# A decode attention and FFN kernel on one core: values of one unit loaded before the FFN's weights, an FFN that is column-tiled throughout and leaves the bank of PV after its first layer, and the output turned inside the next key transpose

## Chip, core and metric

The kernel runs on one NeuronCore of a Trainium2 chip. The metric is the device time of one execution in microseconds. The time is about 1.8 us longer than the span of the profile, which goes from the first to the last instruction. In the views below, PE is the matrix engine (TensorE), PEld its loads of weights, DVE the vector engine, ACT the scalar engine, and SP the engine that issues the large loads.

Executions of the kernel before do not all take the same time, so each run has a state, fast or slow. Verdicts compare fast runs alone. Where I quote all runs, I say so.

## The reference, cut to what matters

```python
x  = A_x                                   # (2, 1, 448), bf16
xn = layernorm(x)
q  = (xn @ wq)                             # 16 heads of 256, two to a key/value head
k, v = the last 2048 of 8192 cached rows   # 8 key/value heads, 256 wide, 2 batches
s  = softmax(q k^T / 16) v @ wo            # attention, then the output projection
g  = silu(relu(xn @ w1) @ w2)              # FFN, 448 -> 1792 -> 448
out = x + s * g
```

The operands are read once: keys 16.8 MB, values 16.8, wq and wo 3.7 each, w1 and w2 1.6 each. The profile counts 44.11 MB read from HBM. There is one token per batch, so there is little arithmetic per byte.

## The kernel before

The work is done in four units u (batch u // 2, half of the heads u % 2). Each unit has 4 MiB of keys and 4 MiB of values. Per unit the PE transposes the keys (`do_T`, 16 chunks of four 128x128 transposes, evacuated by DVE and ACT in turn), multiplies them with q (`do_S`), and after a softmax multiplies the probabilities with the values (`do_PV`). Then `attend` scales and turns the result. At the end 128 matmuls with wo form the output (`O` below). K2 means the keys of unit 2, V2 its values. `obk` and the five `tb` are PSUM banks, where PE leaves its results: `obk` takes PV, the FFN and O, the `tb` take the transposed keys.

```python
def load_v(u):
    deps = [st.get(("PV", u - 2))] + ([st["q_mm"]] if u == 1 else [])
    d_v[u] = pr.dma(SP, vbuf[u % 2][:, :], kv_src(u, A_v_cache), deps)
# ... cut
def softmax(u, fill=()):       # meanwhile() emits the next piece of `fill` on the PE
    meanwhile()
    # DVE: row maximum; PE: transpose it (rmT); DVE: maximum over chunks
    meanwhile()
    # DVE copy; PE: broadcast (bias); DVE: shift
    meanwhile()
    # ACT: Exp; PE: transpose the probabilities (Pt); DVE: copy to pt
    meanwhile()
    # PE: sums (gs); DVE: reciprocal rs
# ... cut
def attend(u):                 # DVE: o_sb = obk * rs; PE: turn o_sb; DVE: at_exp
# ... cut
def do_H(u):                   # u = 0, 1: half of the FFN's first layer, 7 matmuls 4 x 448 into obk
# ... relu on DVE; do_hT: 7 transposes into obk; do_F: 56 matmuls 2 x 112 into obk; silu from obk
# ... cut
scores(0)
load_k(2); load_v(1)
softmax(0)
scores(1)
load_k(3)
softmax(1, value_parts(0)); attend(0)
scores(2)
st["w1"] = pr.dma(SP, ..., w1_src, [st["T", 2]])     # cut
st["w2"] = pr.dma(SP, ..., w2_src, [st["T", 2]])     # cut
load_v(2)
softmax(2, value_parts(1)); attend(1)
load_v(3)
scores(3)
# wo in pieces of 12, 12, 4, 2, 2 of its 32 blocks, each after T of unit 3
softmax(3, [lambda: do_H(0), lambda: do_H(1), do_hT, do_F])
for u in (2, 3):
    do_PV(u); attend(u)
# ... O: for j in range(32): four matmuls of block j; then out = O * g + x on DVE, and two stores
```

All large loads go through one queue, in program order, and in the traces they land in that order.

Of the kernel before, what the change touches and what calls it, by code (L numbers as in the profile page):

```python
# [5 lines left out]
BF = mybir.dt.bfloat16  # L6
F32 = mybir.dt.float32
ACT = mybir.ActivationFunctionType
ALU = mybir.AluOpType
AX = mybir.AxisListType  # L10

PE, DVE, ACTE, SP, POOL = "pe", "dve", "act", "sp", "pool"
# [64 lines left out]
def bass_recurrent_scan__sliding_block_cached__dense_activation_relu__decode_kernel(  # L77
# [11 lines left out]
    B, Sq, D = A_x.shape  # L89
    _, HKV, SK, DH = A_k_cache.shape  # L90
# [8 lines left out]
    NU = 4  # L99
    NT = 64  # L100
    NCHUNK = NT // 4
    UW = NT * DH
    SLOTS = 7
    HC = HD // 2
    FC = DFF // 2
    WO_PARTS = [12, 12, 4, 2, 2]
    NCOL = D // 4
# [6 lines left out]
    with es:  # L114
        pr = _Prog(nc, es)

        def named(name, shape, dt):
            return es.enter_context(nc.sbuf_tensor(name, shape, dt))
# [4 lines left out]
        def view(t, off, dims, n=128, p0=0, pstep=1):  # L123
            width = t.shape[1]
            return bass.AP(t, p0 * width + off, [[width * pstep, n]] + dims)

        ident = named("ident", [128, 128], BF)
# [17 lines left out]
        xr = named("xr", [128, SLOTS * 4], BF)  # L145
        q_n = named("q_n", [128, 512], BF)
        qz = named("qz", [128, 2 * NU * 64], BF)
        h_n = named("h_n", [128, FC], BF)
        h_sb = named("h_sb", [128, 28], BF)
        x_c = named("x_c", [128, NCOL], BF)  # L150
        ea = named("ea", [128, NCOL], F32)
# [30 lines left out]
        def kv_src(u, cache):  # L182
            b, v = divmod(u, 2)
            return cache[b, 4 * v:4 * v + 4, SK - W:SK, :].rearrange("h (r t) d -> r h (t d)", t=NT)
# [16 lines left out]
        def load_k(u):  # L201
            d_k[u] = pr.dma(SP, kbuf[u % 2][:, :], kv_src(u, A_k_cache), [st.get(("T", u - 2))])

        def load_v(u):
            deps = [st.get(("PV", u - 2))] + ([st["q_mm"]] if u == 1 else [])
            d_v[u] = pr.dma(SP, vbuf[u % 2][:, :], kv_src(u, A_v_cache), deps)

        load_k(0)
        d_wq = pr.dma(SP, wq_sb[:, 0:SLOTS * HC], wq_src)
# [19 lines left out]
            out=sd[0:B, 0:1], in0=st2[0:B, 1:2], scalar1=EPS, scalar2=None, op0=ALU.add), [v_ag])  # L229
        a_sd = pr.op(ACTE, lambda e: e.activation(sd[0:B, 1:2], sd[0:B, 0:1], ACT.Sqrt), [v_ve])  # L230
        v_rs = pr.op(DVE, lambda e: e.reciprocal(rstd[0:B, :], sd[0:B, 1:2]), [a_sd])
        for e2 in range(2):
            v_xn = pr.op(DVE, lambda e, e2=e2: e.tensor_scalar(  # L233
                out=view(xg, 128 - 127 * e2, [[256, 4], [128, 2], [2, 64]], n=B),
                in0=view(x_sb, 3 * e2, [[1, 4], [0, 2], [SLOTS, 64]], n=B),
                scalar1=st2[0:B, 0:1], scalar2=rstd[0:B, 0:1],
                op0=ALU.subtract, op1=ALU.mult), [v_rs])
# [22 lines left out]
        def mm(out_ap, lhsT, rhs, start, stop=False, **kw):  # L260
            return lambda e: e.matmul(out_ap, lhsT=lhsT, rhs=rhs, start=start, stop=stop,  # L261
                                      skip_group_check=True, **kw)
# [30 lines left out]
        def do_S(u, g):  # L293
            deps = [st["q"]] + ([st.get(("shift", u - 1))] if g == 0 else [])
            for par in range(2):
                lo = 64 * (2 * u + par) + 24 - 8 * g
                for i in range(4):
                    o = pr.op(PE, mm(sbk[32 * i:32 * i + 32, :], qz[:, lo:lo + 32], view(kt[4 * g + i], par, [[2, 512]]),
                                     g == 0 and par == 0, g == 3 and par == 1, tile_position=(0, 32 * i)),
                              deps + [evac[NCHUNK * u + 4 * g + i]])  # L300
                    deps = []
            for i in range(4):
                last_S[NCHUNK * u + 4 * g + i] = o
            st["S", u] = o
# [48 lines left out]

        def do_PV(u, gs=range(4)):
            bank, src, p = obk, vbuf[u % 2], pt[u % 2]
            deps = [d_v[u], st["pt", u], a_z, st["obk"]]
            for g in gs:
                for a in range(2):
                    for i in range(4):
                        lo = (16 * g + 4 * i + 2 * a) * DH  # L360
                        o = pr.op(PE, mm(bank[32 * i:32 * i + 16, :],
                                         p[:, 256 * a + 64 * i + 16 * g:256 * a + 64 * i + 16 * g + 16], src[:, lo:lo + 2 * DH],
                                         g == 0 and a == 0, g == 3 and a == 1, tile_position=(0, 32 * i)), deps)
                        deps = []
            st["PV", u] = o

        def attend(u):
            b, v = divmod(u, 2)
            ob = st["obk"] = pr.op(DVE, lambda e: e.tensor_scalar(  # L369
                out=o_sb[:, :], in0=obk[:, :], scalar1=rs[:, u:u + 1], scalar2=None, op0=ALU.mult),  # L370
                [st["PV", u], st["rs", u], st.get(("oT", u - 1))])
            deps = [ob, v_fold, st["mbk"]]
            for dhi in range(2):
                for tp in range(2):
                    o = pr.op(PE, mm(mbk_ap(136 + 8 * dhi, 8), o_sb[:, 256 * tp + 128 * dhi:256 * tp + 128 * dhi + 128],
                                     fold[:, 8 * tp:8 * tp + 8], tp == 0, tp == 1), deps)
                    deps = []
            st["oT", u] = o
            st["at", u] = st["mbk"] = pr.op(DVE, lambda e: e.tensor_tensor(
                out=view(at_exp, 128 * b + 64 * v, [[8, 8], [4, 2], [1, 4]]),  # L380
                in0=view(mbk, 136, [[1, 8], [8, 2], [0, 4]]),
                in1=view(qmask, 0, [[0, 8], [0, 2], [1, 4]]), op=ALU.mult), [o, v_qm])
# [21 lines left out]
                        view(qz, 256 * b + 64 * r + 24, [[128, 2], [2, 4], [1, 2]]),  # L404
                        view(mb16, 128 * r + b, [[2, 2], [32, 4], [256, 2]])), [o, p_qz])

        def do_H(u):
            deps = [st["w1"], a_z, st["obk"]]
            for s in range(SLOTS):
                lo = s * FC + u * (FC // 2)  # L410
                o = pr.op(PE, mm(obk[0:4, 0:FC // 2], xr[:, 4 * s:4 * s + 4], w1_sb[:, lo:lo + FC // 2],
                                 s == 0, s == SLOTS - 1), deps)
                deps = []
            st["h_n"] = st["obk"] = pr.op(DVE, lambda e: e.tensor_scalar(  # L414
                out=h_n[0:4, u * (FC // 2):(u + 1) * (FC // 2)], in0=obk[0:4, 0:FC // 2],
                scalar1=0.0, scalar2=None, op0=ALU.max), [o])

        def do_hT():
            deps = [st["h_n"]]
            for j in range(7):  # L420
                o = pr.op(PE, mm(obk[:, 4 * j:4 * j + 4], view(h_n, j, [[7, 128]], n=4), ident[0:4, 0:4], j == 0), deps)
                deps = []
            st["hT"] = st["obk"] = pr.op(DVE, lambda e: e.tensor_copy(
                view(h_sb, 0, [[2, 7], [14, 2], [1, 2]]), view(obk, 0, [[4, 7], [2, 2], [1, 2]])), [o])

        def do_F():
            deps = [st["w2"], st["hT"]]
            for f in range(14):
                for i in range(4):
                    lo = W2_AT + f * D + i * NCOL  # L430
                    o = pr.op(PE, mm(obk[32 * i:32 * i + B, 0:NCOL], h_sb[:, 2 * f:2 * f + 2], w2_sb[:, lo:lo + NCOL],
                                     f == 0, f == 13, tile_position=(0, 32 * i)), deps)
                    deps = []
            a_e = pr.op(ACTE, lambda e: e.activation(ea[:, :], obk[:, 0:NCOL], ACT.Exp, scale=-1.0), [o])
            v_d = pr.op(DVE, lambda e: e.tensor_scalar(
                out=ea[:, :], in0=ea[:, :], scalar1=1.0, scalar2=None, op0=ALU.add), [a_e])
            v_rc = pr.op(DVE, lambda e: e.reciprocal(tmp[:, :], ea[:, :]), [v_d])  # L437
            st["g"] = st["obk"] = pr.op(DVE, lambda e: e.tensor_tensor(
                out=g_sb[:, :], in0=obk[:, 0:NCOL], in1=tmp[:, :], op=ALU.mult), [v_rc])

        def scores(u):
            for i in range(NCHUNK):
                do_T(u, i)
                if u and i >= 6 and i % 4 == 2:
                    do_S(u, (i - 6) // 4)
            if u == 0:
                do_q()
                for g in range(3):
                    do_S(u, g)
            do_S(u, 3)  # L450

        def value_parts(u):
            return [lambda g=g: do_PV(u, (g,)) for g in range(4)]

        scores(0)
        load_k(2)
        load_v(1)
        softmax(0)
        scores(1)
        load_k(3)  # L460
        softmax(1, value_parts(0))
        attend(0)
        scores(2)
        st["w1"] = pr.dma(SP, w1_sb[:, 0:W2_AT], w1_src, [st["T", 2]])
        st["w2"] = pr.dma(SP, w2_sb[:, W2_AT:W2_AT + 14 * D].rearrange("p (hf f) -> p hf f", hf=2), w2_src,
                          [st["T", 2]])
        load_v(2)
        softmax(2, value_parts(1))
        attend(1)
        load_v(3)  # L470
        scores(3)
        d_wo = []
        j0 = 0
        for n in WO_PARTS:
            d_wo.append((j0, pr.dma(SP, wo_sb[:, j0 * D:(j0 + n) * D], wo_src[:, j0 * D:(j0 + n) * D], [st["T", 3]])))
            j0 += n
        softmax(3, [lambda: do_H(0), lambda: do_H(1), do_hT, do_F])
        for u in (2, 3):
            do_PV(u)
            attend(u)  # L480
        for b in range(2):
            m_at = pr.op(PE, mm(mbk_ap(256 + 32 * b, 32), at_exp[:, 128 * b:128 * b + 128],
                                fold[:, :], True, True), [st["at", NU - 1], v_fold, st["mbk"]])
# [4 lines left out]
        for j in range(32):  # L488
            deps = deps + [landed.get(j)]
            for i in range(4):  # L490
# [3 lines left out]
                deps = []  # L494
# [38 lines left out]
```

## Time and profile before

| before | us |
|---|---|
| first timed runs | 116.78, 112.79, 112.93 (median 112.93) |
| profiled run (slow) | 116.5, span 114.7 |

The first lines of the page of the kernel before. The rows are 40 equal slices of the span. PE and DMA are busy tenths, PEclk is the granted TensorE clock in tenths.

```profile
span 114.7 us, 1850 instructions
...
PE   0010399966259999656999965699996525879390
...
PEclk9999999999955799996569999656999998555555
DMA  5889999989899899899898998999898998998000
```

The DMA engines are at least 80% busy from the second slice to the 37th. PE is not, and its clock falls to half four times.

The end of the chain of waits (the work that ended last, in order of time; columns are start, length, what):

```profile
97.85 3.62 PE obk L261 x31
...
101.49 0.76 DVE o_sb L369
...
102.57 3.55 PE obk L261 x27
...
106.14 0.76 DVE o_sb L369
...
108.54 3.18 PE obk L261 x128
```

This is PE work and DVE work end to end: PV of unit 2 (97.85), its output scale (101.49), PV of unit 3 (102.57), its scale, then O from 108.54. No load is in this end of the chain.

The DMA stream, by stretches (columns: stretch and its length, busy time of each engine with the number of instructions, granted clock, DMA share, GB/s):

```profile
4.00:40.00 36.00, 21.64 (x180) 17.75 (x180) 15.90 (x40) 13.64 (x16) 0.00 (x0) 0.91 1.01 437
40.00:80.00 40.00, 33.27 (x286) 23.69 (x282) 19.92 (x41) 15.43 (x19) 0.00 (x0) 0.83 1.01 432
80.00:100.00 20.00, 14.06 (x178) 8.16 (x174) 9.38 (x21) 4.91 (x8) 0.00 (x0) 0.92 0.97 414
...
104.00:105.00 1.00, 1.00 (x12) 0.29 (x8) 0.00 (x0) 0.00 (x0) 0.00 (x0) 0.50 0.98 378
105.00:106.00 1.00, 1.00 (x12) 0.14 (x4) 0.00 (x0) 0.00 (x0) 0.00 (x0) 0.50 0.66 247
106.00:107.00 1.00, 0.14 (x6) 0.05 (x2) 0.75 (x1) 0.00 (x0) 0.00 (x0) 0.50 0.30 113
```

The DMA share is near 1.0 for a hundred microseconds. It falls only from 105 us on, and the last bytes come between 106 and 107.

From the start of each issue and its time to landing, K2 lands at 52.3, V1 at 62.0 and K3 at 71.7 us: 4.19 MB every 9.7 us, that is 432 GB/s. V2 lands at 89.0, V3 at 98.7 and the last piece of wo at about 107.4 (issued at 87.7, 19.7 us to landing). So two things end almost together in this kernel: the stream at 107.4, and the PE chain that reaches O at 108.5. The five loads of wo in the timeline, and the last two of them in the page's list (KB each, us from issue to landing):

```profile
85.89 2.24 SPq L36 DMA_DIRECT2D kbuf<-in_A_wo_dram  x5
...
kbuf<-in_A_wo_dram SPq DMA_DIRECT2D x2, 224.0 KB, 19.7
```

### The profile page before, as it was taken

What the parts mean: (1) busy time and instruction counts of PE and PEld (TensorE: products, weight loads), DVE (VectorE), ACT (ScalarE), POOL (GpSimd) and SP (SyncE); (2) the same over time, 40 slices, a digit from 0 to 9 for tenths busy, and PEclk for the clock granted to TensorE, in tenths of its full rate; (3) what the DMA queues carried; (4) which work ended last, traced back from release to release, by engine and by line L of the source; (5) the groups of instructions that cost most, each with busy time, mean ns of one, the idle gap of its engine ahead of it and who ended that gap; (6) DMA issues with size and microseconds to landing.
All of it is one profiled execution on the core that took longest, in us unless ns stands there. A gap on an engine that the chain in (4) does not pass through costs nothing.

```text
span 114.7 us, 1850 instructions
## 1 busy us (share of the span) xinstructions
PE 78.0 (68%) x810; PEld 54.3 (47%) x810; DVE 49.0 (43%) x111; ACT 35.5 (31%) x42; POOL 2.0 (2%) x11
## 2 busy tenths in 40 slices
PE   0010399966259999656999965699996525879390
PEld 0000399922149776124977612497772224322280
DVE  2091046852623555535445553544553465030401
ACT  1900047960023766020376602036670021000000
POOL 6000000000000000000000000000000000000000
PEclk9999999999955799996569999656999998555555
DMA  5889999989899899899898998999898998998000
GB/s 172 377 366 446 423 480 390 456 366 543 366 411 503 366 469 446 360 514 403 377 514 377 440 468 339 409 493 428 377 520 377 423 491 345 399 409 338 34 6 1
DMA packets 2475, 44.22 MB, mean 385 GB/s; under 512 B 290, under 2 KB 548, under 8 KB 932
## 3 DMA queue, kind: packets, MB, share of 16 engines
q1 hardware_dynamic: 2440, 44.11, 90.4%
q8 instruction: 6, 0.10, 0.3%
q10 hardware_dynamic: 28, 0.00, 0.0%
q14 instruction: 1, 0.01, 0.0%
HBM read 44.11 MB, written 0.00 MB: 385 GB/s over the span
## 4 chain that ended last, share of the span: by engine, by line
PE 64%; DVE 18%; DMA 11%; ACT 3%; issue 2%
PE tb L281 35%; PE obk L261 14%; DMA kbuf<-in_A_k_cache_dram 11%; PE sbk L261 8%; PE mbk L261 4%; DVE s_sb L331 3%; ACT e_sb L336 3%; DVE o_sb L369 2%; DVE rm L314 2%; DVE kt L289 2%; PE mbk L341 2%; DVE h_n L414 1%; PE mbk L319 1%; DVE mrow L322 1%; DVE tmp L437 1%
## 5 line engine op out<-in xcount | busy, mean ns | idle before, releaser
L281 PE MATMUL tb<-ident_f,kbuf 128*128 128x128 f32 x256 | 40.9, 331 | 5.5 <-DMA kbuf<-in_A_k_cache_dram 5.5
L281 PEld LDWEIGHTS tb<-ident_f,kbuf 128*128 128x128 f32 x256 | 38.0, 176 | 9.6 <-DMA kbuf<-in_A_k_cache_dram 5.6
L291 ACT ACTIVATE kt<-tb 128x1024 bf16<-128x1024 bf16 x28 | 27.7, 1023 | 32.2 <-PE tb L281 32.2
L289 DVE COPY kt<-tb 128x1024 bf16<-128x1024 bf16 x36 | 24.8, 691 | 26.4 <-PE tb L281 26.4
L261 PE MATMUL obk<-vbuf,pt 128*16 128x512 bf16 x128 | 12.5, 504 | 1.6 <-DVE rs L351 1.6
L261 PE MATMUL sbk<-kt,qz 128*32 128x512 bf16 x128 | 11.0, 393 | 1.6 <-DVE kt L289 1.1
L336 ACT ACTIVATE e_sb<-s_sb 128x512 bf16<-128x512 f32 x4 | 2.5, 629 | 24.7 <-DVE s_sb L331 24.7
L261 PEld LDWEIGHTS obk<-vbuf,pt 128*16 128x16 bf16 x128 | 3.3, 105 | 6.0 <-issue 5.0
L369 DVE TENSOR_SCALAR o_sb<-obk,rs 128x512 bf16<-128x512 f32 x4 | 3.0, 742 | 7.0 <-PE obk L261 7.0
L341 PE MATMUL mbk<-ident,e_sb 128*128 128x128 bf16 x16 | 1.8, 243 | 5.7 <-ACT e_sb L336 5.7
L261 PE MATMUL mbk<-ident,xg 2*128 2x2 bf16 x7 | 0.3, 163 | 7.4 <-DVE xg L233 7.4
L261 PEld LDWEIGHTS sbk<-kt,qz 128*32 128x32 bf16 x128 | 2.7, 94 | 5.6 <-issue 2.1
L341 PEld LDWEIGHTS mbk<-ident,e_sb 128*128 128x128 bf16 x16 | 1.0, 106 | 6.9 <-ACT e_sb L336 6.9
L314 DVE TENSOR_REDUCE rm<-sbk 128x4 f32<-128x512 f32 x4 | 2.7, 686 | 3.6 <-PE sbk L261 3.6
L319 PE MATMUL mbk<-ident_f,rm 128*1 128x128 f32 x4 | 1.1, 270 | 4.3 <-DVE rm L317 4.3
L346 DVE COPY pt<-mbk 128x512 bf16<-128x512 bf16 x4 | 1.7, 424 | 5.1 <-PE mbk L341 5.1
L261 PEld LDWEIGHTS mbk<-ident,xg 2*128 2x128 bf16 x7 | 0.3, 100 | 7.4 <-DVE xg L233 7.4
L261 PE MATMUL mbk<-fold,o_sb 128*128 128x8 bf16 x16 | 1.1, 173 | 3.5 <-DVE o_sb L369 3.5
L261 PEld LDWEIGHTS mbk<-fold,o_sb 128*128 128x128 bf16 x16 | 0.7, 108 | 5.5 <-DVE o_sb L369 5.5
L261 PE MATMUL obk<-kbuf,at 128*2 128x112 bf16 x128 | 3.2, 298 | 0.3 <-DVE at L484 0.3
L319 PEld LDWEIGHTS mbk<-ident_f,rm 128*1 128x1 f32 x4 | 0.3, 79 | 6.3 <-DVE rm L317 6.3
L261 PEld LDWEIGHTS obk<-kbuf,at 128*2 128x2 bf16 x128 | 2.9, 124 | 0.4 <-DVE at L484 0.4
(67 smaller groups left out, 41.9 us busy)
## 6 DMA issues: line engine op xcount, KB each, us to landing
kbuf<-in_A_k_cache_dram SPq DMA_DIRECT2D x4, 4096.0 KB, 27.8
vbuf<-in_A_v_cache_dram SPq DMA_DIRECT2D x4, 4096.0 KB, 32.0
vbuf<-in_A_wq_dram SPq DMA_DIRECT2D x1, 3584.0 KB, 20.3
kbuf<-in_B_w_dram SPq DMA_DIRECT2D x2, 1568.0 KB, 11.5
kbuf<-in_A_wo_dram SPq DMA_DIRECT2D x2, 1344.0 KB, 17.5
kbuf<-in_A_wo_dram SPq DMA_DIRECT2D x1, 448.0 KB, 19.6
kbuf<-in_A_wo_dram SPq DMA_DIRECT2D x2, 224.0 KB, 19.7
x_c<-in_A_x_dram ACTq DMA_DIRECT2D x2, 0.9 KB
```

The source lines that it names most:

```text
L261: return lambda e: e.matmul(out_ap, lhsT=lhsT, rhs=rhs, start=start, stop=stop, skip_group_check=True, **kw)
L281: o = pr.op(PE, lambda e, n=n, lo=lo: e.matmul(bank_f[:, n * 128:(n + 1) * 128], lhsT=src_f[:, lo:lo + 128], rhs=ident_f[:, :], start=True ...
L289: evac[n_th] = pr.op(DVE, lambda e: e.tensor_copy(dst[:, :], bank[:, :]), deps)
L291: evac[n_th] = pr.op(ACTE, lambda e: e.activation(dst[:, :], bank[:, :], ACT.Copy), deps)
L314: v = pr.op(DVE, lambda e: e.tensor_reduce(out=rm4[:, :], in_=view(sbk, 0, [[1, 4], [4, 128]]), axis=AX.X, op=ALU.max), [st["S", u]])
L319: m = st["rmT", u] = pr.op(PE, lambda e: e.matmul(mbk_ap(0, 128, 1), lhsT=rm[:, :], rhs=ident_f[:, :], start=True, stop=True, is_transpose ...
L322: v = pr.op(DVE, lambda e: e.tensor_reduce(out=mrow[0:1, :], in_=view(mbk, 0, [[1, 8], [8, 16]], n=1), axis=AX.X, op=ALU.max, negate=True) ...
L331: v = st["shift", u] = pr.op(DVE, lambda e: e.scalar_tensor_tensor(out=view(s_sb, 0, [[4, 128], [1, 4]]), in0=view(sbk, 0, [[4, 128], [1, ...
L336: a = st["exp", u] = pr.op(ACTE, lambda e: e.activation(e_sb[:, :], s_sb[:, :], ACT.Exp, accum_out=ssum[:, 0:1]), [v, st.get(("Pt", u - 1) ...
L341: o = pr.op(PE, lambda e, j=j: e.matmul(mb16[:, 512 + 128 * j:640 + 128 * j], lhsT=e_sb[:, 128 * j:128 * j + 128], rhs=ident[:, :], start= ...
L346: v = st["pt", u] = pr.op(DVE, lambda e: e.tensor_copy(view(pt[u % 2], 0, [[256, 2], [16, 16], [8, 2], [1, 8]]), view(mb16, 512, [[256, 2] ...
L369: ob = st["obk"] = pr.op(DVE, lambda e: e.tensor_scalar(out=o_sb[:, :], in0=obk[:, :], scalar1=rs[:, u:u + 1], scalar2=None, op0=ALU.mult) ...
```

## The change

The intent was to shorten the PE chain after the last keys. V2 is loaded before w1 and w2, so that PV of unit 2 can fill the gaps of softmax 3, as PV of units 0 and 1 fill those of softmax 1 and 2. The FFN moves behind that softmax. Its first layer and its transposes become column-tiled (four groups of 32 columns side by side, as the second layer already was). The first layer stays in `obk`, but the transposes and the second layer go to two of the `tb` banks, so that the silu runs beside PV of unit 3. V3 comes in two loads. The turn of units 0 and 1 moves behind the fourth chunk of the next T, so that T need not wait for the output scale. An early dummy Exp moves the load of the Exp table.

```diff
-        def load_v(u):
+        def load_v(u, cuts=(0, NT)):        # one DMA per cut; do_PV waits for the one it needs
...
+        pr.op(ACTE, lambda e: e.activation(tmp[0:B, 0:1], st2[0:B, 0:1], ACT.Exp), [a_sd])
...
-        def attend(u):
+        def attend_scale(u):                # DVE part
+        def attend_turn(u):                 # PE turn and at_exp
...
-        def do_H(u):                        # 7 matmuls 4 x 448, called twice
+        def do_H():                         # 28 matmuls 4 x 224, tile_position=(0, 32 * i)
...                                          # do_hT into tb[0], do_F into tb[1], not into obk
         def scores(u):
             for i in range(NCHUNK):
                 do_T(u, i)
...
+                if i == 3 and u > 1:
+                    attend_turn(u - 2)
...
-        def value_parts(u):
-            return [lambda g=g: do_PV(u, (g,)) for g in range(4)]
+        def values(u):
+            return [lambda gs=gs: gs and do_PV(u, gs) for gs in ((0,), (), (1, 2), (3,))]
...
-        softmax(1, value_parts(0))
-        attend(0)
+        softmax(1, values(0))
+        attend_scale(0)
+        load_v(2)
         scores(2)
         st["w1"] = ...; st["w2"] = ...
-        load_v(2)
-        softmax(2, value_parts(1))
-        attend(1)
-        load_v(3)
+        softmax(2, values(1))
+        attend_scale(1)
+        load_v(3, (0, 48, 64))
         scores(3)
...
-        softmax(3, [lambda: do_H(0), lambda: do_H(1), do_hT, do_F])
-        for u in (2, 3):
-            do_PV(u)
-            attend(u)
+        softmax(3, values(2))
+        attend_scale(2)
+        do_H()
+        attend_turn(2)
+        do_hT()
+        do_F()
+        do_PV(3)
+        attend_scale(3)
+        attend_turn(3)
```

More of the change, by code (lines that the diff above doesn't have):

```diff
@@ L147, in bass_recurrent_scan__sliding_block_cached__dense_activation_relu__decode_kernel @@
         qz = named("qz", [128, 2 * NU * 64], BF)
-        h_n = named("h_n", [128, FC], BF)
+        h_n = named("h_n", [128, FC // 4], BF)
         h_sb = named("h_sb", [128, 28], BF)
@@ L202, in load_k @@
             d_k[u] = pr.dma(SP, kbuf[u % 2][:, :], kv_src(u, A_k_cache), [st.get(("T", u - 2))])
-        def load_v(u):
-            deps = [st.get(("PV", u - 2))] + ([st["q_mm"]] if u == 1 else [])
-            d_v[u] = pr.dma(SP, vbuf[u % 2][:, :], kv_src(u, A_v_cache), deps)
+        def load_v(u, cuts=(0, NT)):
+            deps = [None if u == 0 else st["q_mm"] if u == 1 else st["PV", u - 2]]
+            d_v[u] = []
+            for lo, hi in zip(cuts, cuts[1:]):
+                d_v[u].append((hi, pr.dma(SP, vbuf[u % 2][:, lo * DH:hi * DH],
+                                          kv_src(u, A_v_cache)[:, :, lo * DH:hi * DH], deps)))
         load_k(0)
@@ L355, in do_PV @@
             bank, src, p = obk, vbuf[u % 2], pt[u % 2]
-            deps = [d_v[u], st["pt", u], a_z, st["obk"]]
             for g in gs:
+                deps = [next(d for hi, d in d_v[u] if hi >= 16 * g + 16), st["pt", u], a_z, st["obk"]]
                 for a in range(2):
@@ L365, in do_PV @@
             st["PV", u] = o
-        def attend(u):
-            b, v = divmod(u, 2)
-            ob = st["obk"] = pr.op(DVE, lambda e: e.tensor_scalar(
+        def attend_scale(u):
+            st["osb", u] = st["obk"] = pr.op(DVE, lambda e: e.tensor_scalar(
                 out=o_sb[:, :], in0=obk[:, :], scalar1=rs[:, u:u + 1], scalar2=None, op0=ALU.mult),
                 [st["PV", u], st["rs", u], st.get(("oT", u - 1))])
-            deps = [ob, v_fold, st["mbk"]]
+        def attend_turn(u):
+            b, v = divmod(u, 2)
+            deps = [st["osb", u], v_fold, st["mbk"]]
             for dhi in range(2):
@@ L405, in do_q @@
                         view(mb16, 128 * r + b, [[2, 2], [32, 4], [256, 2]])), [o, p_qz])
-        def do_H(u):
+        def do_H():
             deps = [st["w1"], a_z, st["obk"]]
             for s in range(SLOTS):
-                lo = s * FC + u * (FC // 2)
-                o = pr.op(PE, mm(obk[0:4, 0:FC // 2], xr[:, 4 * s:4 * s + 4], w1_sb[:, lo:lo + FC // 2],
-                                 s == 0, s == SLOTS - 1), deps)
-                deps = []
+                for i in range(4):
+                    lo = s * FC + i * (FC // 4)
+                    o = pr.op(PE, mm(obk[32 * i:32 * i + 4, 0:FC // 4], xr[:, 4 * s:4 * s + 4], w1_sb[:, lo:lo + FC // 4],
+                                     s == 0, s == SLOTS - 1, tile_position=(0, 32 * i)), deps)
+                    deps = []
             st["h_n"] = st["obk"] = pr.op(DVE, lambda e: e.tensor_scalar(
-                out=h_n[0:4, u * (FC // 2):(u + 1) * (FC // 2)], in0=obk[0:4, 0:FC // 2],
-                scalar1=0.0, scalar2=None, op0=ALU.max), [o])
+                out=h_n[:, :], in0=obk[:, 0:FC // 4], scalar1=0.0, scalar2=None, op0=ALU.max), [o])
         def do_hT():
-            deps = [st["h_n"]]
+            hbk = tb[0][:, :].bitcast(F32).tensor
+            deps = [st["h_n"], evac[NU * NCHUNK - 4]]
             for j in range(7):
-                o = pr.op(PE, mm(obk[:, 4 * j:4 * j + 4], view(h_n, j, [[7, 128]], n=4), ident[0:4, 0:4], j == 0), deps)
-                deps = []
-            st["hT"] = st["obk"] = pr.op(DVE, lambda e: e.tensor_copy(
-                view(h_sb, 0, [[2, 7], [14, 2], [1, 2]]), view(obk, 0, [[4, 7], [2, 2], [1, 2]])), [o])
+                for i in range(4):
+                    o = pr.op(PE, mm(view(hbk, 4 * j, [[1, 4]], n=32, p0=32 * i), view(h_n, j, [[7, 32]]),
+                                     ident[:, 32 * i:32 * i + 4], j == 0, tile_position=(0, 32 * i)), deps)
+                    deps = []
+            st["hT"] = pr.op(DVE, lambda e: e.tensor_copy(
+                view(h_sb, 0, [[2, 7], [14, 2], [1, 2]]), view(hbk, 0, [[4, 7], [2, 2], [1, 2]])), [o])
         def do_F():
-            deps = [st["w2"], st["hT"]]
+            fbk = tb[1][:, :].bitcast(F32).tensor
+            deps = [st["w2"], st["hT"], evac[NU * NCHUNK - 3]]
             for f in range(14):
@@ L430, in do_F @@
                     lo = W2_AT + f * D + i * NCOL
-                    o = pr.op(PE, mm(obk[32 * i:32 * i + B, 0:NCOL], h_sb[:, 2 * f:2 * f + 2], w2_sb[:, lo:lo + NCOL],
+                    o = pr.op(PE, mm(view(fbk, 0, [[1, NCOL]], n=B, p0=32 * i), h_sb[:, 2 * f:2 * f + 2], w2_sb[:, lo:lo + NCOL],
                                      f == 0, f == 13, tile_position=(0, 32 * i)), deps)
                     deps = []
-            a_e = pr.op(ACTE, lambda e: e.activation(ea[:, :], obk[:, 0:NCOL], ACT.Exp, scale=-1.0), [o])
+            f_ap = view(fbk, 0, [[1, NCOL]])
+            a_e = pr.op(ACTE, lambda e: e.activation(ea[:, :], f_ap, ACT.Exp, scale=-1.0), [o])
             v_d = pr.op(DVE, lambda e: e.tensor_scalar(
@@ L437, in do_F @@
             v_rc = pr.op(DVE, lambda e: e.reciprocal(tmp[:, :], ea[:, :]), [v_d])
-            st["g"] = st["obk"] = pr.op(DVE, lambda e: e.tensor_tensor(
-                out=g_sb[:, :], in0=obk[:, 0:NCOL], in1=tmp[:, :], op=ALU.mult), [v_rc])
+            st["g"] = pr.op(DVE, lambda e: e.tensor_tensor(
+                out=g_sb[:, :], in0=f_ap, in1=tmp[:, :], op=ALU.mult), [v_rc])
         def scores(u):
@@ L443, in scores @@
                 do_T(u, i)
-                if u and i >= 6 and i % 4 == 2:
+                if i >= 6 and i % 4 == 2:
                     do_S(u, (i - 6) // 4)
-            if u == 0:
-                do_q()
-                for g in range(3):
-                    do_S(u, g)
+                if i == 3 and u > 1:
+                    attend_turn(u - 2)
             do_S(u, 3)
-        def value_parts(u):
-            return [lambda g=g: do_PV(u, (g,)) for g in range(4)]
-        scores(0)
+        def values(u):
+            return [lambda gs=gs: gs and do_PV(u, gs) for gs in ((0,), (), (1, 2), (3,))]
+        for i in range(NCHUNK):
+            do_T(0, i)
+        do_q()
+        for g in range(4):
+            do_S(0, g)
         load_k(2)
```

## The prediction

> **What bounds the kernel now.** Two things, nearly level.
>
> (a) The PE chain. The chain of waits is 64% PE and 18% DVE. After the third T it runs: last score 87.24 us, softmax 3 with the FFN in its gaps to 97.8, PV2 3.6, output scale and turn 1.1, PV3 3.6, tail 2.4, O projection 108.54 to 111.72, then 3.0 us to the end of the span (114.7).
>
> (b) The DMA stream. In the table of stretches the DMA share is 0.93 to 1.05 from 4 to 105 us (44.1 MB): never dry. By issue plus time to landing, the 4 MiB loads land every 9.7 us (K2 52.3, V1 62.0, K3 71.7, V2 89.0, V3 98.7), 432 GB/s. The Trainium skill, "DMA: Bandwidth & Descriptors", Specifications, gives a fabric ceiling of 435 GB/s; the trace agrees. The last piece of wo lands at about 107.4 us, 1.1 us before the O projection starts.
>
> The profiled run (116.5 us) is slow; two of three timed runs took 112.8 and 112.9. Granted clock is 0.66 over 30:40, 50:60 and 70:80, and 0.5 from 96.7. The Trainium skill, "TensorE: Matmul & The Clock Gate", Part 1, says the clock gate judges free-running windows of about 3.4 us; the transitions here are multiples of 3.41 us apart. I read the slow state as an unlucky phase, which lengthens (a) and not (b). Then the fast runs' O projection ends near 108.0 (112.9 less 1.8 outside the span less 3.0): already close to the landing of wo.
>
> **What the change does.**
> - Turn inside T: twice, reciprocal, scale and turn (52.63 to 53.80; 72.60 to 73.77) leave the PE chain: -1.2 us each, +0.3 for the turn inside T. About -1.8.
> - V2 before w1, w2: V2 lands at 81 instead of 89, so PV2 fits in softmax 3's gaps as PV0 and PV1 do; softmax 3 then takes 5.5 us (67.07 to 72.60) where it took 10.5. PV2's 3.6 us leaves the chain.
> - FFN after that, column-tiled: H 1.3 to 1.5 (two halves of 1.49 before), relu about 0.35, hT 0.5, copy 0.2, F 0.85. About 3.5 on the chain, but the silu (1.7 us) now runs beside PV3.
> - V3 in two pieces: three quarters land at about 96.3, all at 98.7.
> - Exp table early: the load (1.28 us at 23.6) already sat in ACT idle time. Zero.
> - PV regrouped: zero.
>
> Sum: S3 ends 85.4, softmax 91, FFN 95.1, PV3 end about 99.7, O start about 102: chain (a) is some 6 us shorter.
>
> **Critical path.** Same bytes, queue still full: the stream still ends at about 107.4. O starts early and stalls on its wo pieces. After the last lands: 8 matmuls (0.3), 3.0 to the end, 1.8 outside: about 112.5. Gain over the fast before: 0.4 us; over its slow runs: 4.
>
> **Predicted: 112.4 us, 111.7 to 113.0 in 8 of 10.** Faster by over 2%: 0.05; within 2%: 0.93; slower: 0.02. No slow state.
>
> **Signs.** PE waits on the wo DMA in the O projection, 3 to 5 us in total; the chain ends DMA, O, DVE; T right behind the gs matmul; PV2 before the FFN; no silu in the chain; the last wo landing within 0.5 us of 107.4.
>
> **What would make it wrong.** The stream is faster in fast runs[...];[...] the FFN or V3 pushing O past 104, so that PE ends last.

## The result

| | before | after |
|---|---|---|
| median, all runs of the comparison | 112.86 us (112.67 to 116.78, 4 runs) | 112.84 us (112.67 to 112.93, 4 runs) |
| ratio of fast runs, after over before | | 1.0002, 95% interval 0.9982 to 1.0023 |
| profiled run | slow, span 114.7 | fast, span 110.9 |

A ratio is the mean time of one kernel's fast runs over the mean of the other's fast runs of the same rounds, so it is not quite the ratio of the medians quoted beside it. The outputs are correct.

The page after:

```profile
span 110.9 us, 1921 instructions
...
PE   0010299995428999859999949699985464293480
...
PEclk9999999999995589995899995799999985555555
DMA  3988979898899889889989998998999999999920
```

The end of its chain of waits:

```profile
83.07 24.39 DMA kbuf<-in_A_wo_dram
...
107.50 0.39 PE obk L265 x8
...
107.91 0.28 DVE tmp L513
...
108.22 0.27 DVE out_sb L515
```

PE work of any length is gone from the end of the chain. It now ends in one piece of 24 us, the stream of wo from its issue to 107.46 us. Eight matmuls (the two last blocks) and two DVE operations follow.

What PE does before that, from the timeline after (start, length, engine, line, operation, shapes, and in brackets the idle time before and what ended it):

```profile
71.67 1.97 PE L285 MATMUL tb<-ident_f,kbuf 128*128 128x128 f32 x16 [0.90 <-DMA kbuf<-in_A_k_cache_dram]
...
87.73 0.38 PE L265 MATMUL mbk<-ssum,gsum 128*128 128x1 f32 x2
...
89.11 0.84 PE L265 MATMUL obk<-kbuf,xr 128*4 128x224 bf16 x28 [1.00 <-DVE o_sb L372]
...
91.38 1.47 PE L265 MATMUL tb<-kbuf,h_sb 128*2 128x112 bf16 x56 [0.39 <-DVE h_sb L432]
...
96.35 3.59 PE L265 MATMUL obk<-vbuf,pt 128*16 128x512 bf16 x32 [3.49 <-DMA vbuf<-in_A_v_cache_dram]
...
98.78 0.24 PEld L265 LDWEIGHTS obk<-vbuf,pt 128*16 128x16 bf16 x8 [0.61 <-DMA vbuf<-in_A_v_cache_dram]
...
102.38 1.29 PE L265 MATMUL obk<-kbuf,at 128*2 128x112 bf16 x48 [0.29 <-DVE at L502]
...
105.29 2.01 PE L265 MATMUL obk<-kbuf,at 128*2 128x112 bf16 x72 [1.62 <-DMA kbuf<-in_A_wo_dram]
...
107.50 0.36 PE L265 MATMUL obk<-kbuf,at 128*2 128x112 bf16 x8 [0.20 <-DMA kbuf<-in_A_wo_dram]
```

PE now waits for data at three stages. T of unit 3 waits 0.90 us for K3. PV of unit 3 waits 3.49 us for three quarters of V3, and its last weights wait 0.61 us for the rest (98.78). O starts at 102.38, six microseconds earlier than in the profile before, stops after 48 matmuls (12 blocks) at 103.7, and waits 1.62 us for the second piece of wo. PE is idle for wo during 1.62 and 0.20 us, 1.8 us in all. O's matmuls are busy for 3.66 us at half clock, and in the profile before for 3.18 us, also at half clock; the 0.5 us more is not explained.

The stretches of the DMA after, to be set beside those of before:

```profile
4.00:40.00 36.00, 21.80 (x172) 18.48 (x172) 15.44 (x39) 13.12 (x17) 0.00 (x0) 0.91 1.01 437
40.00:80.00 40.00, 35.62 (x337) 22.63 (x339) 23.02 (x45) 18.64 (x22) 0.00 (x0) 0.91 1.00 429
80.00:100.00 20.00, 12.19 (x210) 5.66 (x209) 6.71 (x19) 2.10 (x5) 0.00 (x0) 0.77 1.00 421
...
104.00:105.00 1.00, 0.00 (x0) 0.00 (x0) 0.00 (x0) 0.00 (x0) 0.00 (x0) 0.50 0.95 369
105.00:106.00 1.00, 0.71 (x36) 0.71 (x40) 0.00 (x0) 0.00 (x0) 0.00 (x0) 0.50 0.75 269
106.00:107.00 1.00, 1.00 (x50) 0.67 (x40) 0.00 (x0) 0.00 (x0) 0.00 (x0) 0.50 0.34 127
```

They are nearly the same: share 1.0 to 100 us, then 0.75 and 0.34 in the last two microseconds. The stream carries the same 44.11 MB at the same rate and ends at the same time, whatever PE does.

### The profile page after: what moved, and what is told of

Same layout as the page of the kernel before. It is cut to its first block, busy times and chain, and to the rows that moved or that the text cites. A ratio compares the mean times of both kernels' runs of the same rounds, so it can differ in the third digit from the quotient of the medians.

```text
span 110.9 us, 1921 instructions
## 1 busy us (share of the span) xinstructions
PE 74.0 (67%) x845; PEld 49.7 (45%) x845; DVE 48.0 (43%) x110; ACT 35.4 (32%) x43; POOL 1.9 (2%) x11
## 3 DMA queue, kind: packets, MB, share of 16 engines
q1 hardware_dynamic: 2584, 44.11, 93.5%
HBM read 44.11 MB, written 0.00 MB: 398 GB/s over the span
## 4 chain that ended last, share of the span: by engine, by line
DMA 56%; PE 34%; DVE 4%; SPq 2%; issue 1%; ACT 1%
DMA kbuf<-in_A_k_cache_dram 34%; PE tb L285 25%; DMA kbuf<-in_A_wo_dram 22%; PE sbk L265 5%; PE obk L265 2%; SPq L36 2%; PE mbk L265 1%; DVE s_sb L335 1%; ACT e_sb L340 1%; DVE rm L318 1%; DVE q_n L399 1%; PE mbk L345 1%; DVE pt L350 0%; DVE qz L409 0%; PE mbk L403 0%
## 5 line engine op out<-in xcount | busy, mean ns | idle before, releaser
L285 PE MATMUL tb<-ident_f,kbuf 128*128 128x128 f32 x256 | 36.6, 306 | 6.3 <-DMA kbuf<-in_A_k_cache_dram 6.3
L285 PEld LDWEIGHTS tb<-ident_f,kbuf 128*128 128x128 f32 x256 | 33.5, 161 | 10.4 <-DMA kbuf<-in_A_k_cache_dram 6.4
L265 PE MATMUL obk<-vbuf,pt 128*16 128x512 bf16 x128 | 13.5, 529 | 3.5 <-DMA vbuf<-in_A_v_cache_dram 3.5
L265 PE MATMUL obk<-kbuf,at 128*2 128x112 bf16 x128 | 3.7, 292 | 2.1 <-DMA kbuf<-in_A_wo_dram 1.8
L265 PE MATMUL mbk<-one_f,mall 1*128 1x1 f32 x8 | 1.6, 268 | 2.5 <-DVE mall L330 2.5
L335 DVE SCALAR_TENSOR_TENSOR s_sb<-sbk,bias,low 128x512 f32<-128x512 f32 x4 | 3.0, 751 | 0.1
## 6 DMA issues: line engine op xcount, KB each, us to landing
kbuf<-in_B_w_dram SPq DMA_DIRECT2D x2, 1568.0 KB, 23.6
```

Source lines behind the costliest of these rows:

```text
L265: return lambda e: e.matmul(out_ap, lhsT=lhsT, rhs=rhs, start=start, stop=stop, skip_group_check=True, **kw)
L285: o = pr.op(PE, lambda e, n=n, lo=lo: e.matmul(bank_f[:, n * 128:(n + 1) * 128], lhsT=src_f[:, lo:lo + 128], rhs=ident_f[:, :], start=True ...
L335: v = st["shift", u] = pr.op(DVE, lambda e: e.scalar_tensor_tensor(out=view(s_sb, 0, [[4, 128], [1, 4]]), in0=view(sbk, 0, [[4, 128], [1, ...
```

## The experiments

Theory A: after the change the stream of loads sets the time; PE has slack, and the kernel before was held by the same stream in its fast runs, or nearly. Rival B: PE and DVE still set the time, and the chain was not really shortened (or lost elsewhere what it gained).

### The kernel before, again, over many runs (b_again, b_look)

No edit.

> The kernel before, unchanged, to see its fast state in a profile and its states over many runs. Theory A (the fast runs of before were already held by the DMA stream, the slow ones by the PE chain in an unlucky phase of the clock gate): in a fast profile the last piece of wo lands at 107.2 to 107.6 us, the O projection ends within 0.6 us of that, and fast runs lie at 112.6 to 113.0 us; slow runs, if any, show the same landing of wo and a later start of O. Rival B (the fast runs of before are held by the PE chain, and that the two kernels tie is chance): the O projection ends more than 1 us after the last landing, with no wait on a wo load.

> The kernel before once more, only for a profile that may fall in a fast run. Theory A, as the runs so far leave it: if it is fast, with a mean clock of 0.87 or more, the last wo piece lands at 107.2 to 107.6 us, the O projection starts between 102 and 105 us instead of 108.5, and its end is within 1 us of the landing. If it is slow again it is the profile already seen.

Neither profile fell in the best state. b_again took 113.3 to 116.8 us (six runs) and its profile was slow, at 116.79 us. b_look took 113.72 us. The end of its chain of waits:

```profile
96.38 3.62 PE obk L261 x29
...
101.10 3.55 PE obk L261 x26
...
107.02 1.77 PE obk L261 x128
```

O ran from 107.02 to 108.79 without a wait, at full clock (1.77 us, where the slow profile had 3.18). The last wo piece landed at about 107.5 (issued at 86.2, 21.3 us to landing), over 1 us before O's end. So this run, as rival B has it, was still held by PE, though its O ended only 0.9 us later than that of the changed kernel (107.89). I had expected O to start between 102 and 105 us; that was wrong for this run.

The same kernel against itself gave 1.0072, interval 1.0001 to 1.0142, because its runs lie between the states. So below, small differences are taken from the changed kernel's steadier times.

The timed runs tell more. The kernel before ran 33 times beside the experiments, and seven times more as b_again and b_look. All 40 runs, by the mean granted clock of the run:

| mean granted clock | runs | time, us |
|---|---|---|
| 0.832 to 0.833 | 10 | 116.46 to 117.04 |
| 0.844 to 0.864 | 8 | 113.34 to 114.88 |
| 0.876 | 4 | 113.18 to 113.38 |
| 0.882 to 0.886 | 11 | 112.65 to 113.00 |
| 0.892 to 0.901 | 7 | 112.78 to 113.59 |

The time roughly follows the clock, and stops at about 112.7. The median of the 40 is 113.4 us.

### The changed kernel, again (a_again)

No edit.

> The changed kernel, unchanged, beside many runs of before on the same chip, since before's runs spread from 112.7 to 116.9 us in the last batch while every run of the changed kernel so far lay within 0.3 us. Theory A (stream-bound): all runs 112.6 to 113.0 us whatever their mean granted clock. Rival B: as many runs as before's lie above 113.3.

Six runs, 112.82 to 112.96 us, at mean clocks from 0.832 to 0.876. With the four runs of the comparison that makes ten between 112.67 and 112.96. At a clock of 0.832, where before takes 116.4 or more, the changed kernel takes 112.88. Against before's fast runs of the same rounds the ratio is 0.9975 (0.9949 to 1.0002). Over these clocks the changed kernel's time does not depend on the clock, as theory A has it.

### 2.1 us of delay on the chain (a_d3, b_d3)

```diff
         do_PV(3)
+        for _ in range(3):          # in before: in the loop, for u == 3
+            st["delay"] = pr.op(DVE, lambda e: e.tensor_reduce(
+                out=rm4[:, :], in_=view(sbk, 0, [[1, 4], [4, 128]]), axis=AX.X, op=ALU.max),
+                [st["S", 3], st["PV", 3], st.get("delay")])
         attend_scale(3)             # in before: attend(3)
```

> The changed kernel with three idle reductions of about 0.7 us each put on the DVE between PV3 and the output scale (2.1 to 2.3 us more on the PE and DVE chain, same bytes). Theory A: the O projection starts at about 104.6 instead of 102.4 and still ends where the last wo piece lets it; time +0.0 to +0.2 us (112.8 to 113.0). Rival B (the chain still sets the time): +2.1 to +2.3 us, 115.0.

> The same three reductions in the kernel before, between PV3 and its output scale. Theory A: before has at most about 1 us of slack in its fast state, so +1.2 to +2.3 us (114.0 to 115.2); what is missing from 2.2 us is its slack. If before had as much slack as after, +0 to +0.2 us, and the change would have moved nothing even in the chain.

The changed kernel took 112.82 us (112.72 to 113.18), the same as without the delay. Its timeline shows the delay and where it went:

```profile
100.07 2.14 DVE L498 TENSOR_REDUCE rm<-sbk 128x4 f32<-128x512 f32 x3 [3.65 <-PE obk L265]
102.13 0.74 DVE L372 TENSOR_SCALAR o_sb<-obk,rs 128x512 bf16<-128x512 f32 x1
...
104.50 2.97 PE L265 MATMUL obk<-kbuf,at 128*2 128x112 bf16 x120 [0.29 <-DVE at L506]
...
107.67 0.36 PE L265 MATMUL obk<-kbuf,at 128*2 128x112 bf16 x8 [0.20 <-DMA kbuf<-in_A_wo_dram]
```

The three reductions took 2.14 us, O started at 104.50 instead of 102.38, and its last eight matmuls still waited for wo. The slack is at least 2.1 us, and rival B (115.0) is out.

The kernel before took 114.03 and 114.25 us in its two fast runs, about 1.3 us more than its best runs (112.7 to 112.9), and up to 119.2 us in the others. That is inside what theory A gave it (114.0 to 115.2): by the difference it had some 0.8 us of slack in these two. That is rough: their clocks (0.894 and 0.909) are not those of its best runs (0.882 to 0.886).

### A shorter stream (a_wo24, a_cut24, b_cut24)

The last 8 of the 32 blocks of wo are not loaded; matmuls of other blocks stand in, so the result is meant to be wrong. (The comparison reported it within its tolerance all the same: it does not tell this change in wo from rounding.)

```diff
-    WO_PARTS = [12, 12, 4, 2, 2]
+    WO_PARTS = [12, 12]             # a_wo24;   [8, 8, 4, 2, 2] in a_cut24 and b_cut24
...
-                lo = j * D + i * NCOL
+                lo = (j % 24) * D + i * NCOL    # a_wo24;   max(j - 8, j % 8 if j < 8 else 0) * D in the others,
+                                                # and each block's wait for its piece moves by 8
```

> The changed kernel with the last 8 of 32 blocks of wo not loaded (0.92 MB less, which at 432 GB/s is 2.1 us of the stream; the O projection reads blocks 0 to 7 again in their place, result wrong on purpose; same matmuls). Theory A: the stream ends about 2.1 us earlier and so does the kernel: 110.5 to 111.0 us. Rival B: no change, 112.8.

It took 112.22 us (ratio to before's fast runs 0.9921), 0.6 us less and not 2.1. The expectation was wrong, and the timeline says why:

```profile
102.34 0.76 PE L265 MATMUL obk<-kbuf,at 128*2 128x112 bf16 x48 [0.29 <-DVE at L502]
...
105.29 2.04 PE L265 MATMUL obk<-kbuf,at 128*2 128x112 bf16 x80 [2.19 <-DMA kbuf<-in_A_wo_dram]
```

The stream did end 2.2 us earlier, but its last load was now a piece of 12 blocks, and 80 matmuls (2.04 us) had to wait for it. With the small last pieces restored:

> The shorter stream again, better made than in a_wo24, where the two large pieces left 20 of 32 blocks to be multiplied after the last landing: 24 blocks of wo in pieces 8, 8, 4, 2, 2, and the last piece read last (result wrong on purpose, same matmuls). Theory A: the last piece lands at 105.2 to 105.5 us and the kernel follows, 110.5 to 111.0 us, 1.9 to 2.2 less than the changed kernel. Rival B: 112.8.

> The same shorter stream in the kernel before. Theory A: its PE chain is nearly as long as the stream in its best runs and longer in the others, so it gains at most 0.5 us in the best runs: 112.3 to 113.0 for the fastest, the others as before. If it falls to 111 as the changed kernel does, the change shortened no chain that matters.

a_cut24 took 110.79 us (110.60 to 110.84), 2.0 us less than the changed kernel, as expected; the ratio to the fast runs of before is 0.9787 (0.9763 to 0.9811, unclear at the 2% line). Its end:

```profile
102.29 3.08 PE L265 MATMUL obk<-kbuf,at 128*2 128x112 bf16 x120 [0.29 <-DVE at L502]
...
105.58 0.35 PE L265 MATMUL obk<-kbuf,at 128*2 128x112 bf16 x8 [0.21 <-DMA kbuf<-in_A_wo_dram]
```

O's last eight matmuls start at 105.58, 1.9 us before the 107.50 of the changed kernel: the kernel follows its stream. With the same cut the kernel before took 110.70, 113.26, 113.42, 114.68, 116.58 and 117.02 us. Five of six runs gained nothing, as expected. One did, at a mean clock of 0.906; I had expected at most 0.5 us there. So with a lucky clock the old chain too is about 2 us shorter than the full stream. This is more than the 0.8 us of b_d3; what the old chain has to spare differs from run to run, and these few runs do not settle how much.

### Is it the clock that spreads the kernel before? (b_warm)

The kernel before with 62 matmuls of 128x128 by 512 into an idle bank, placed in PE's gaps; their results are never read.

```diff
+        def warm(u, n):
+            spare = tb[(NCHUNK * (u + 1)) % NTB][:, :].bitcast(F32)
+            deps = [p_id, p_qz, evac.get(NCHUNK * (u + 1) - NTB)]
+            for _ in range(n):
+                pr.op(PE, mm(spare, ident[:, :], qz[:, :], True, True), deps)
+        warm(-1, 11)                # before the first T; 3 to 16 more in each softmax and attend
```

> The kernel before, with 128x128 by 512 matmuls into an idle PSUM bank put into the gaps of the PE, so that the clock gate sees more work (result right, same bytes). If before's spread is the clock gate's phase acting on a PE-bound chain: T runs at full clock, mean clock above 0.93, and the times draw in towards the stream's 112.7 to 113.2 us. If something else makes the spread: 112.7 to 116.9 as before. If the extra matmuls get in the chain's way, some part of them shows in the chain and the test says little.

It took 112.89 us (112.71 to 113.35, six runs), with mean clocks of 0.944 to 0.965. The clock row of its page, and the end of its chain of waits:

```profile
PEclk9999999999999999999999999859999999679955
```

```profile
84.38 23.18 DMA kbuf<-in_A_wo_dram
...
107.61 0.39 PE obk L261 x8
```

The chain of the kernel before, without any of the change, now ends as the changed kernel's does, in the wo stream at 107.56 us. So the kernel before was held by its chain at half clock; with a higher clock the same program order is short enough. That its best runs without these matmuls also end at the stream is inferred from this and from their floor of 112.65 us; no profile fell in one of them. The extra matmuls are 18.9 us of PE time by the list of groups, and none of it shows in the time.

### Parts of the change undone (a_unsplit, a_order)

```diff
-        load_v(3, (0, 48, 64))
+        load_v(3)                   # a_unsplit
```

> The changed kernel with V3 in one load again. PV3 then starts at the landing of all of V3 (98.8) instead of three quarters (96.35) and ends about 2.4 us later, at 102.4; O starts at 104.8 instead of 102.4. Theory A: the wo stream still ends the kernel, 112.8 to 113.1 us. Rival B: +2.4 us, 115.2.

112.83 us (112.73 to 112.88): no change. O started at 104.77 us instead of 102.38, and its last eight matmuls at 107.54, right after the last piece of wo. Splitting V3 shortens the chain but buys nothing here. In a_order `load_v(2)` moves back behind the loads of w1 and w2:

> The changed kernel with w1 and w2 ahead of V2 again. V2 lands at 89 instead of 81.4, its first PV group then holds the PE queue from about 82 to 89, and softmax 3 with all that follows moves by 6 to 7 us: O would start at 105.3 to 106.5 and needs 3.2 us. Theory A: the 4.5 us of slack hide most of it, 113.2 to 114.2 us. Rival B: 119. If the order costs nothing at all (112.8), the slack is larger than I think.

113.86 us (112.76 to 113.99):

```profile
89.18 1.03 PE L265 MATMUL obk<-vbuf,pt 128*16 128x512 bf16 x8 [6.42 <-DMA vbuf<-in_A_v_cache_dram]
...
106.78 2.40 PE L265 MATMUL obk<-kbuf,at 128*2 128x112 bf16 x128 [0.29 <-DVE at L502]
```

The first PV group held PE for 6.42 us until V2 came, and O started at 106.78 instead of 102.38 (expected 105.3 to 106.5). The time rose by 1.0 us in the median: four runs took 113.84 to 113.99 us (clocks of 0.840 to 0.848), and two, with a clock of 0.862, took 112.76 and 112.91, which is no loss. The expectation for the time holds in the four: most of a 6.4 us hold disappears in the slack that the waits for V3 and wo gave. That the time goes with the clock again fits a chain with so little slack left. Of the two parts undone, the order of the loads is the one that showed in the time; the turn inside T, the move of the FFN and the early Exp were not undone one by one.

### An attempt at the stream itself (a_k8)

```diff
-    WO_PARTS = [12, 12, 4, 2, 2]
+    WO_PARTS = [4, 12, 12, 2, 2]    # and the first piece as 16 loads of 8 partitions each (28 KB), awaited together
```

> An attempt at the stream itself. In the last 1.5 us of every trace the DMA share falls to 0.75 and then 0.34: some of the 16 DMA engines still have work while the others are done. Here the first 4 blocks of wo come in 16 loads of 8 partitions each, which I expect to be spread over half the engines only, so that the other half ends 1.1 us earlier. If the late engines are in the unloaded half: last landing at 107.0, time 112.3 to 112.6. If some of them are in the loaded half: last landing at 108.5, time 113.8 to 114.1. If the loads are spread over all engines: 112.8.

116.58 us (116.51 to 116.73), outside all three cases.

```profile
90.00:95.00 5.00, 3.05 (x116) 2.47 (x116) 1.47 (x6) 0.26 (x1) 0.00 (x0) 0.79 0.93 400
95.00:100.00 5.00, 2.74 (x24) 0.70 (x24) 1.34 (x3) 0.00 (x0) 0.00 (x0) 0.53 1.04 319
100.00:105.00 5.00, 1.78 (x30) 0.78 (x30) 1.37 (x4) 0.00 (x0) 0.00 (x0) 0.81 0.99 332
...
108.00:110.00 2.00, 0.08 (x4) 0.00 (x0) 0.00 (x0) 0.00 (x0) 0.00 (x0) 0.50 0.31 123
```

Between 95 and 105 us, when the rest of V3 and the small loads landed (100.2 and 104.3 us), the stream moved 319 and 332 GB/s (the changed kernel 416 and 404 in the same stretches) with the DMA share at about 1.0, and its end moved to 110. In the packed trace the 128 packets of the small loads (3584 bytes each) took 219 ns on average, where the packets of this size in the changed kernel (its piece of 4 blocks) took 142 ns. Besides, O waited until 110.0 for the second piece of 12 blocks, with 64 matmuls (1.7 us) still to do. So the small loads cost far more than the unevenness they were to level. That such loads use half of the engines was a guess, which no view here shows; which engines are the late ones, and why these loads are slow, stays open. None of the runs gave a kernel faster than both with a right result on the full data.

## Why the prediction was right

The forecast was 112.4 us, 111.7 to 113.0, and within 2%; the result is 112.84.

- **The stream as the floor.** Right. The last piece of wo landed at 107.46 us (forecast 107.4), and a_d3, a_unsplit and a_cut24 show that the time follows the stream and not the chain. The time came out 0.4 us above the forecast: its own sum was 112.5, the trace has 3.4 us from the landing to the end of the span (107.46 to 110.9) where I took 3.3, and the median lies 0.2 us above the profiled run of 112.67.
- **The chain.** Right in its end, O at 102.38 (forecast about 102), but partly by luck. The last score came at 82.6 us (forecast 85.4) and the FFN ended at 92.85 (forecast 95.1); PE then waited 3.5 us for V3, whose landing at 96.3 was forecast well. This landing put O where it was, not the sum of the chain. V2 landed before its first PV group was due and softmax 3 took 5.5 us, from the last score at 82.6 to the sums at 88.1, as forecast. The FFN from the end of the output scale to its last matmul took 3.9 us (88.96 to 92.85) instead of 3.5; the 56 matmuls of its second layer took 1.47 us at half clock, not 0.85.
- **Waits on PE.** Mis-sized. I forecast 3 to 5 us of waits on wo; they were 1.8. O began about when I said, so the reason is O's own length: from 102 to 107.7 us is 5.7 us, which leaves 3.9 us of waits at full clock (1.77 us of matmuls in b_look), but only 2.0 with the 3.66 us at half clock that it had. The waits for V3 (3.5 and 0.6 us) and for K3 (0.9 us), in which the chain had already lost part of its gain, I did not list. The turn inside T did start T behind the sums for unit 2 (53.75 us, no wait), but for unit 3 the gain went into the wait for K3.
- **The Exp table.** Right: the load stood in idle time before (23.6 us, when the next Exp was at 31.6), and at 5.9 us it stands in idle time again, since the first T starts at 13.1. No run tests it alone.
- **The slow state.** "No slow state" held in all ten runs of the changed kernel. The reading behind it (an unlucky phase of the clock gate, that is of what sets PE's granted clock, lengthens the chain and leaves the stream alone) was an argument then. b_warm shows that a higher clock, with the program otherwise as it was, takes most of the spread away (112.71 to 113.35 us). That the phase of its windows decides which clock a run gets was not tested.
- **Before's fast runs "already close to the landing of wo".** Right for the best runs only, and inferred there. Of the 40 runs, 12 lie between 112.65 and 113.00; other fast runs go up to 114.9. The clean tie of 1.0002 owes something to luck: the three fast runs of before in it were all among the best.

## What to carry to other kernels

Before shortening a chain, ask when the last byte lands that it needs, and how much work must follow it: if the queue never runs dry, the chain's gain ends there, however many microseconds the timeline shows. Give the last load of a stream a small piece, since all that waits for it comes after it (a_wo24 kept 0.6 us of a gain that was 2.0 in a_cut24). A chain that is shorter than the stream still buys something, steady times: here it took the granted clock out of the sum.

## What the Trainium skill lacked or had wrong

- "DMA: Bandwidth & Descriptors", Where 436 GB/s comes from, says that for transfers between HBM and SBUF the HBM side (about 358 GB/s) binds. With one core at work it did not: 432 GB/s over each 4 MiB load, close to the 435 of the fabric that Specifications gives. The page's own remark that its measurements are of a single core fits; the warning should say so too.
- "TensorE: Matmul & The Clock Gate", Part 1, says for modelling that the ramp penalty is under 1% of a typical kernel's span. This figure is not for a kernel like this one, whose clock falls again in its gaps, a case that the same Part describes further down without a pointer from the figure. In the kernel before the time spread from 112.65 to 117.04 us, 3.9%, and filling the gaps with unread matmuls removed most of it (112.71 to 113.35).
- The same page does not say which matmuls count as activity. In the profile before, PE was busy through PV and O with 16 and 2 stationary columns and the granted clock stayed at 0.5 to the end; 62 matmuls with 128 columns raised the mean to 0.944 and more. In b_look the clock did rise before O, to 0.91 from 105 to 106 us and to 1.0 after. What the gate counts is open.
- "ScalarE: Activation LUTs", What ACT_TABLE_LOAD costs, gives 1283 ns for the load and 1380 ns more for a drain. The load is 1283 ns in the trace after, but the next activation starts right behind it (load at 2.49 us, activation at 3.78), and the next load right behind that activation (its end at 4.36, load at 4.38): no drain is to be seen there.
- No page has the cost of a load cut into 16 loads of 8 partitions in the middle of a full stream: 319 and 332 GB/s in a_k8, where the changed kernel moved 416 and 404 in the same stretches (95 to 100 and 100 to 105 us).
